# A transformer block whose first phase begins seven heads on half of the hidden dimension, with the shift joined later as a bias

## The chip, the cores and the metric

The kernel runs on one core of a Trainium2 chip. The metric is the device time of one execution in microseconds (us), lower is better. Every run of this document counts as fast by the rule that sorts slow executions out (no run was over 1.5% above the fastest of its kernel), so all comparisons are between fast runs. The differences here are a few tenths of a per cent, so the runs come in rounds of five, beside nine runs of the kernel before on the same chip.

Engines in the profile are PE (TensorE, matmuls), PEld (its weight loads), DVE (VectorE), ACT (ScalarE), POOL (GpSimd) and SP (which issues the loads here).

## The reference

One block of a transformer with modulation, in bf16: S = 2048 rows, D = 1024, 32 query heads on 4 key/value heads of 128, the last 512 keys only, and a gated FFN of 3584.

```python
mod = (silu(c) @ w_mod).reshape(1, 6, 1, -1)
sa, ca, ga, sb, cb, gb = ...                     # six vectors of D
h = layernorm(x) * (1 + ca) + sa                 # scale 1 + ca, shift sa
x = x + ga * (attention(h @ wq, k[-512:], v[-512:]) @ wo)
h = layernorm(x) * (1 + cb) + sb
x = x + gb * ((silu(h @ w_gate) * (h @ w_up)) @ w_down)
```

## The kernel before

The rows go in four chunks of 512. For each chunk and head there is a unit of three parts on PE: q (8 matmuls of 128x512), the scores S (4 of the same size, with the exponential on ACT), and the output O (16 of 130 columns, on the unit before). The steady unit takes 3.5 us, without a gap on PE. The change touches only what comes ahead of the first units: loading x, the scale (`ca1` = 1 + ca) and shift (`sa`), the first layernorm, and the q of the first heads.

```python
for tt in range(QT): load_x(tt)                  # 4 tiles of x, 256 KB each
for half in range(DH):                           # halves of D
    load_wm(1, half)                             # w_mod of the scale, 1 MB
    load_wm(0, half)                             # w_mod of the shift, 1 MB
    load_wq(0, 0, (half,))                       # Wq of heads 0-3, half of D, 1 KB rows
# ... K, V, then load_wq(0, 1): heads 4-7
warm(16)                                         # matmuls on constants, to raise the clock
# ... SiLU of c, on ACT and DVE

def mod_cols(vec, half, dst, add_one):           # 512 values of one vector
    ps = mm("mod_ps", (P, 4))
    for i in range(4):
        for dt in range(DT):                     # 32 matmuls with ONE moving column
            nc.tensor.matmul(ps[:, i:i + 1], lhsT=wm[:, dt, i * P:(i + 1) * P],
                             rhs=siluc[:, dt:dt + 1], start=(dt == 0), stop=(dt == DT - 1))
    # ... to dst on DVE

LEAD = 3
for t in range(QT):
    ln_stats(t); n = ln_norm(t, t % 2 == 0)      # statistics on DVE, norm on ACT or DVE
    # 8 transposes of n into PSUM (h0_ps)
    warm(2)
for half in range(DH):
    mod_cols(1, half, ca1, True)
    mod_cols(0, half, sa, False)
    for dt in range(4 * half, 4 * half + 4):     # h = n * ca1 + sa, out of PSUM
        ln_affine(("h1", 0), dt, h0_ps[half][:, dt % 4, :], ca1, sa, dt % 2 == 0)
    # this half's 4 of the 8 q matmuls, for LEAD heads
# ...
for k in range(NU + 1):                          # units
    # loads of Wq are issued 8 heads ahead
    emit_s(k); emit_q(k + LEAD); run_tasks(k); emit_o(k - 1)
```

No program order is forced on the engines in this phase, apart from the warm-up matmuls; a scheduler places the instructions. In the trace of before, the warm-up matmuls up to 5.7 us are 0.427 us apart from start to start, and those after it 0.216: that is the rise of the clock.

Of the kernel before, what the change touches and what calls it, by code (L numbers as in the profile page):

```python
# [8 lines left out]
ACT = mybir.ActivationFunctionType  # L9
# [579 lines left out]
def fast_path(ctx, tc, flag, A_x, A_k_cache, A_v_cache, A_wq, A_wo, B_x, B_w_gate, B_w_up,  # L589
# [41 lines left out]
    hpool = ctx.enter_context(tc.tile_pool(name="hT", bufs=4))  # L631
    pa_ = ctx.enter_context(tc.tile_pool(name="blkA", bufs=8))
    pb_ = ctx.enter_context(tc.tile_pool(name="blkB", bufs=7))
    pc_ = ctx.enter_context(tc.tile_pool(name="blkC", bufs=12))
    wk = ctx.enter_context(tc.tile_pool(name="work", bufs=2))
    sm = ctx.enter_context(tc.tile_pool(name="small", bufs=4))
    psp = ctx.enter_context(tc.tile_pool(name="psum", bufs=4, space=bass.MemoryType.PSUM))
# [28 lines left out]
    def load(out, in_):  # L666
        with nc.allow_non_contiguous_dma(reason="weight slice"):
            fetch(out=out, in_=in_)

    nc.scalar.preload_act_table_set("natural_log_exp_and_others")  # L670


# [16 lines left out]
    def load_wq(cc, hg, parts=(0, 1)):  # L689
        for i in parts:  # L690
            t = blkB("wq", [P, 4, 512])
            load(t, wq_v[:, 4 * i:4 * i + 4, hg * 512:(hg + 1) * 512])
            wq_tiles[(cc, hg, i)] = t

    for tt in range(QT):
        load_x(tt)
    for half in range(DH):
        load_wm(1, half)
        load_wm(0, half)
        load_wq(0, 0, (half,))  # L700
    kT = blkB("kT", [P, Hkv, W])
    for kv in range(Hkv):
        pin(nc.sync.dma_start_transpose(  # L703
# [2 lines left out]
    v_sb = const.tile([P, Hkv, WT, Dh + 32], BF16, name="v_sb")  # L706
    for kv in range(Hkv):
        load(v_sb[:, kv, :, 0:Dh], v_v[:, kv])
    nc.gpsimd.memset(v_sb[:, :, :, Dh:VN], 1.0)
    load_wq(0, 1)  # L710


    ident = const.tile([P, P], BF16, name="ident")
    make_identity(nc, ident)
    ones_bf = const.tile([P, P], BF16, name="ones_bf")
    nc.vector.memset(ones_bf, 1.0)
    eps_t = const.tile([P, 1], FP32, name="eps_t")
    nc.vector.memset(eps_t, eps)

    warm_w = const.tile([P, 512], BF16, name="warm_w")  # L720
    nc.gpsimd.memset(warm_w, 0.5)
    warm_ps = mm("warm_ps")

    def warm(n):
        for _ in range(n):
            tc.keep_in_program_order(
                nc.tensor.matmul(warm_ps, lhsT=ones_bf, rhs=warm_w, start=True, stop=True))

    warm(16)
    modT = const.tile([P, 4, DT], FP32, name="modT")  # L730
    sa, ca1, sb, cb1 = (modT[:, i, :] for i in range(4))
    ga_bc = const.tile([P, D], FP32, name="ga_bc")
    gb_bc = const.tile([P, D], FP32, name="gb_bc")


    ec = wk.tile([DT, P], FP32, name="ec", tag="f32", bufs=2)
    nc.scalar.activation(out=ec, in_=c_r, func=ACT.Exp, scale=-1.0)
    nc.vector.tensor_scalar(out=ec, in0=ec, scalar1=1.0, scalar2=None, op0=ALU.add)
    rc = wk.tile([DT, P], FP32, name="rc", tag="f32", bufs=2)
    nc.vector.reciprocal(out=rc, in_=ec)  # L740
    sil_r = const.tile([DT, P], BF16, name="sil_r")
    nc.vector.tensor_tensor(out=sil_r, in0=c_r, in1=rc, op=ALU.mult)
    sil_ps = mm("sil_ps", (P, DT), BF16)
    nc.tensor.transpose(sil_ps, sil_r, ident[0:DT, 0:DT])
    siluc = const.tile([P, DT], BF16, name="siluc")
    nc.vector.tensor_copy(out=siluc, in_=sil_ps)

    def mod_cols(vec, half, dst, add_one):
        wm = wm_tiles.pop((vec, half))
        ps = mm("mod_ps", (P, 4))  # L750
        for i in range(4):
            for dt in range(DT):
                nc.tensor.matmul(ps[:, i:i + 1], lhsT=wm[:, dt, i * P:(i + 1) * P],
                                 rhs=siluc[:, dt:dt + 1], start=(dt == 0), stop=(dt == DT - 1))
        nc.vector.tensor_scalar(out=dst[:, 4 * half:4 * half + 4], in0=ps,  # L755
                                scalar1=1.0 if add_one else 0.0, scalar2=None, op0=ALU.add)






# [144 lines left out]
            at(k + 11 + dt, ln_mod, key, dt, sc, sh)  # L907


    LEAD = 3  # L910
    qT = {}

    def put_q(g, q_ps):
        t = wk.tile([P, TCW], BF16, name="qT", tag="row", bufs=5)
        nc.vector.tensor_copy(out=t, in_=q_ps)  # L915
        qT[g] = t



    new_hT(("h1", 0))  # L920
    h0_ps = [big("h0_ps", (P, 4, TCW), BF16) for _ in range(2)]
    for t in range(QT):
        ln_stats(t)
        n = ln_norm(t, t % 2 == 0)
        for dt in range(DT):
            nc.tensor.transpose(h0_ps[dt // 4][:, dt % 4, t * P:(t + 1) * P],
                                n[:, dt * P:(dt + 1) * P], ident)
        warm(2)
    q0_ps = []
    for half in range(DH):  # L930
        mod_cols(1, half, ca1, True)
        mod_cols(0, half, sa, False)
        for dt in range(4 * half, 4 * half + 4):
            ln_affine(("h1", 0), dt, h0_ps[half][:, dt % 4, :], ca1, sa, dt % 2 == 0)
        if half == 0:
            q0_ps = [mm("q_ps") for _ in range(LEAD)]
        for n in range(4 * LEAD):
            dt, g = (4 * half + n // LEAD, n % LEAD) if half == 0 else (4 + n % 4, n // 4)
            nc.tensor.matmul(q0_ps[g],
                             lhsT=wq_tiles[(0, 0, dt // 4)][:, dt % 4, g * P:(g + 1) * P],  # L940
                             rhs=hT[("h1", 0)][:, dt, :], start=(dt == 0), stop=(dt == DT - 1))
    for g in range(LEAD):
        put_q(g, q0_ps[g])

    k_ld = []
    NSQ = 2 * 2 * (H // 4)
# [24 lines left out]
                                               accum_out=kk[:, i:i + 1]))  # L971

    def bound_mod():
        nc.vector.tensor_reduce(out=gd[:, 1:2], in_=kk, axis=AX.X, op=ALU.max)
        c2 = sm.tile([P, DT], FP32, name="c2", tag="c2", bufs=2)
        nc.vector.tensor_tensor(out=c2, in0=ca1, in1=ca1, op=ALU.mult)
        nc.vector.tensor_reduce(out=gd[:, 2:3], in_=c2, axis=AX.X, op=ALU.max)
        s2 = sm.tile([P, DT], FP32, name="s2", tag="c2", bufs=2)
        nc.vector.tensor_tensor(out=s2, in0=sa, in1=sa, op=ALU.mult)
        nc.vector.tensor_reduce(out=gd[:, 3:4], in_=s2, axis=AX.X, op=ALU.add)  # L980

    def bound_final():
        nc.vector.tensor_reduce(out=gd[:, 0:1], in_=sq, axis=AX.X, op=ALU.add)
# [30 lines left out]
    def emit_q(g):  # L1014
        cc, h = divmod(g, H)
        q_ps = mm("q_ps")
        for dt in range(DT):
            nc.tensor.matmul(q_ps,  # L1018
                             lhsT=wq_tiles[(cc, h // 4, dt // 4)][:, dt % 4,
                                                                 (h % 4) * P:(h % 4 + 1) * P],  # L1020
                             rhs=hT[("h1", cc)][:, dt, :], start=(dt == 0), stop=(dt == DT - 1))
        put_q(g, q_ps)

# [114 lines left out]
    for g in range(3, NU, 4):  # L1138
        at(g + 3, xpose_o, g // H, (g % H) // 4)
    for cc in range(1, NTC):  # L1140
        plan_ln((cc - 1) * H + (10 if cc == 1 else 2), ("h1", cc), ca1, sa)
    for cc in range(NTC):
        for q in range(NQ):
            s0 = cc * H + q * HQ + HQ + 5
# [25 lines left out]
    def emit_gu(cc, f):  # L1170
        fg, fi = divmod(f, 4)
        if fi == 0:
            guT[(cc, fg)] = blkA("guT", [P, 4, TCW])
        ps = big("gu_ps")
        for n, nm in enumerate(("wg", "wu")):
            for dt in range(DT):
                nc.tensor.matmul(ps[:, n, :],  # L1177
                                 lhsT=gu_w[(cc, fg, nm, dt // 4)][:, dt % 4, fi * P:(fi + 1) * P],
                                 rhs=hT[("h2", cc)][:, dt, :], start=(dt == 0),
                                 stop=(dt == DT - 1))  # L1180
        g = wk.tile([P, TCW], BF16, name="sg", tag="row", bufs=5)
        nc.scalar.activation(out=g, in_=ps[:, 0, :], func=ACT.Silu)  # L1182
        nc.vector.tensor_tensor(out=guT[(cc, fg)][:, fi, :], in0=ps[:, 1, :], in1=g, op=ALU.mult)  # L1183

# [5 lines left out]
    def emit_down(cc, dh, t, widths=(512,)):  # L1190
        row = (cc * QT + t) * P
        c0 = 0
        for w in widths:
            dsl = slice(dh * 512 + c0, dh * 512 + c0 + w)
            d_ps = mm("d_ps", (P, w))
            for f in range(FT):
                nc.tensor.matmul(d_ps, lhsT=guT[(cc, f // 4)][:, f % 4, t * P:(t + 1) * P],  # L1197
                                 rhs=wd_tiles[(cc, dh, f // 4)][:, f % 4, c0:c0 + w],
                                 start=(f == 0), stop=(f == FT - 1))
            r = wk.tile([P, w], FP32, name="f32", tag="f32", bufs=2)  # L1200
            nc.vector.tensor_tensor(out=r, in0=d_ps, in1=gb_bc[:, dsl], op=ALU.mult)  # L1201
            o = wk.tile([P, w], BF16, name="o_sb", tag="row", bufs=5)
            nc.vector.tensor_tensor(out=o, in0=r, in1=xt[cc * QT + t][:, dsl], op=ALU.add)
            nc.scalar.dma_start(out=out2d[row:row + P, dsl], in_=o)
            c0 += w
# [4 lines left out]

    stage["steps"] = True
    for k in range(NU + 1):
        if k % 4 >= 2 and 4 * (k // 4) + 8 < NU:
            g = 4 * (k // 4) + 8
            load_wq(g // H, (g % H) // 4, (k % 4 - 2,))
        if k < NU:
            emit_s(k)
        if k + LEAD < NU:
            emit_q(k + LEAD)
        if k == NU - 4:  # L1220
            load_gu(0, 0)
        run_tasks(k)
        if k >= 1:
            emit_o(k - 1)
# [63 lines left out]
```

## Time and profile before

| | before |
|---|---|
| median of the runs (first 3; all 6) | 1277.75; 1277.67 us |
| PE busy | 1255.9 of 1275.6 us |
| first q matmul starts | 15.74 us |
| end of the first head's O | 31.3 us |

First the page of the kernel before: PE's busy time, and the shares of the chain that ended last.

```profile
span 1275.6 us, 17906 instructions
...
PE 1255.9 (98%) x7396; PEld 640.6 (50%) x7537; DVE 606.9 (48%) x1325; ACT 333.7 (26%) x433; POOL 1.3 (0%) x10
...
## 4 chain that ended last, share of the span: by engine, by line
PE 96%; SPq 2%; issue 1%; DVE 1%; DMA 0%
```

PE bounds the kernel, and 2% of the chain lies on SP's queue, which issues the loads: early on, PE waited for weights. Where, the timeline of PE shows (start, length, line and operation, how many; in brackets the idle time before and what ended it).

```profile
15.74 1.46 PE L939 MATMUL q_ps<-hT,wq 128*128 128x512 bf16 x6 [1.06 <-ACT hT L852]
...
19.84 0.95 PE L753 MATMUL mod_ps<-siluc,wm 128*128 128x1 bf16 x32 [0.55 <-DMA wm<-in_w_mod_dram]
21.05 1.02 PE L1018 MATMUL q_ps<-hT,wq 128*128 128x512 bf16 x3 [0.26 <-DVE modT L755]
...
28.52 1.04 PE L1018 MATMUL q_ps<-hT,wq 128*128 128x512 bf16 x4 [0.25 <-DMA wq<-in_A_wq_dram]
...
32.02 1.89 PE L1018 MATMUL q_ps<-hT,wq 128*128 128x512 bf16 x8
...
785.48 1.67 PE L1197 MATMUL d_ps<-wd,guT 128*128 128x512 bf16 x7
...
1267.80 1.45 PE L1197 MATMUL d_ps<-wd,guT 128*128 128x128 bf16 x23
```

How to read it: a line's length includes the end of its last matmul, which the next line already overlaps (the line at 32.02 us is 1.89 us long, and the next O starts after 1.73), so rates are read from start to start. Eight 128x512 matmuls from 32.02 to 33.75 us (the next O) take 1.73 us, 0.216 each. From 32.02 us on the kernel is in its steady unit. The needed work done by then is 40 q, 12 S and 16 O matmuls, 12.1 us at the steady rates. The other 19.9 us are what this document calls the lead-in: all time at the start in which PE did no q, S or O. The last two lines, from two short stretches of the timeline (a group is cut off where the stretch begins or ends), are the first matmul of the down projection, and the last group of all, which ends at 1269.25 us. Some records of matmuls are missing in this trace, so its counts fall a little short.

### The profile page before, as it was taken

How to read it: one execution, taken by the hardware profiler on the slowest of the kernel's cores; microseconds unless marked ns; L12 is line 12 of the kernel's file. 1: busy time of each engine (PE TensorE's matmuls, PEld its weight loads, DVE VectorE, ACT ScalarE, POOL GpSimd, SP SyncE). 2: the span in 40 equal slices, each digit the busy share in tenths (PEclk: the TensorE clock that was granted, in tenths of full speed). 3: DMA queues.
4: the chain of work that ended last, by engine and by line, in shares of the span. 5: the costliest groups of instructions: out<-in, count | busy, mean ns of one | idle time of the engine just before them, and what ended most of it. 6: DMA issues, size and time to landing. Idle time of an engine off the chain costs nothing.

```text
span 1275.6 us, 17906 instructions
## 1 busy us (share of the span) xinstructions
PE 1255.9 (98%) x7396; PEld 640.6 (50%) x7537; DVE 606.9 (48%) x1325; ACT 333.7 (26%) x433; POOL 1.3 (0%) x10
## 2 busy tenths in 40 slices
PE   8999999999999999999999999999999999999997
PEld 4555555555555555555554444444444444444444
DVE  4575578867587755576654632321222112221212
ACT  4543334343343433333341111011100111011100
POOL 0000000000000000000000000000000000000000
PEclk9999999999999999999999999999999999999999
DMA  9988556685646563546465367426632565425711
GB/s 276 220 219 212 144 137 182 165 192 148 176 125 168 137 183 107 152 112 145 126 196 147 133 226 199 145 95 211 218 129 81 175 216 189 139 91 182 246 35 35
DMA packets 307868, 204.46 MB, mean 160 GB/s; under 512 B 145601, under 2 KB 305345, under 8 KB 307778
## 3 DMA queue, kind: packets, MB, share of 16 engines
q1 hardware_dynamic: 302866, 199.03, 55.0%
q10 hardware_dynamic: 4912, 4.20, 1.0%
q8 instruction: 61, 1.00, 0.3%
q14 instruction: 29, 0.24, 0.1%
HBM read 165.94 MB, written 4.21 MB: 133 GB/s over the span
## 4 chain that ended last, share of the span: by engine, by line
PE 96%; SPq 2%; issue 1%; DVE 1%; DMA 0%
PE gu_ps L1177 30%; PE a_ps L1095 17%; PE q_ps L1018 17%; PE d_ps L1197 15%; PE o_ps L1063 9%; PE s_ps L1031 8%; SPq L664 1%; SPq L703 1%; DMA wq<-in_A_wq_dram 0%; DVE junk L954 0%; DVE qT L915 0%; DVE junk L786 0%; DVE acc L1103 0%; DVE oq L1050 0%; DVE f L1201 0%
## 5 line engine op out<-in xcount | busy, mean ns | idle before, releaser
L1033 ACT ACTIVATE pT<-s_ps 128x1024 bf16<-128x1024 f32 x256 | 248.9, 1020 | 356.6 <-PE s_ps L1031 228.9
L1095 PE MATMUL a_ps<-wo,oT 128*128 128x512 bf16 x987 | 239.9, 379 | 2.0
L1018 PE MATMUL q_ps<-hT,wq 128*128 128x512 bf16 x999 | 236.7, 379 | 0.6 <-DVE modT L755 0.3
L1183 DVE TENSOR_TENSOR guT<-gu_ps,sg 128x512 bf16<-128x512 f32 x112 | 77.4, 691 | 286.4 <-ACT sg L1182 286.4
L1177 PE MATMUL gu_ps<-hT,wg 128*128 128x512 bf16 x875 | 209.7, 379 | 1.1
L1182 ACT ACTIVATE sg<-gu_ps 128x512 bf16<-128x512 f32 x112 | 66.9, 597 | 488.7 <-PE gu_ps L1177 483.0
L1197 PE MATMUL d_ps<-wd,guT 128*128 128x512 bf16 (+2 forms) x934 | 193.2, 366 | 0.9
L915 DVE CAST qT<-q_ps 128x512 bf16<-128x512 f32 x128 | 88.2, 690 | 158.5 <-PE q_ps L1018 157.7
L1177 PE MATMUL gu_ps<-hT,wu 128*128 128x512 bf16 x659 | 162.0, 379 | 0.7
L1095 PEld LDWEIGHTS <-oT 128*128 128x128 bf16 x1024 | 100.1, 98 | 120.6
L1018 PEld LDWEIGHTS <-wq 128*128 128x128 bf16 x1000 | 97.7, 98 | 118.2 <-DMA wq<-in_A_wq_dram 0.7
L1197 PEld LDWEIGHTS <-guT 128*128 128x128 bf16 x952 | 90.9, 98 | 103.0
L1063 PEld LDWEIGHTS <-pT 128*128 128x128 bf16 x2048 | 126.8, 98 | 31.0 <-issue 0.4
L1177 PEld LDWEIGHTS <-wg 128*128 128x128 bf16 x896 | 87.7, 98 | 105.5
L1063 PE MATMUL o_ps<-v_sb,pT 128*128 128x130 bf16 x2048 | 137.3, 220 | 0.1
L1031 PE MATMUL s_ps<-qT,kT 128*128 128x512 bf16 x467 | 129.3, 379 | 3.0 <-ACT pT L1033 0.6
L1177 PEld LDWEIGHTS <-wu 128*128 128x128 bf16 x672 | 65.7, 98 | 79.3
L1050 DVE TENSOR_TENSOR oq<-o_ps,rl 128x256 bf16<-128x256 f32 (+2 forms) x256 | 100.4, 419 | 3.8 <-issue 0.2
L1201 DVE TENSOR_TENSOR f<-d_ps,gb_bc 128x512 f32<-128x512 f32 (+2 forms) x34 | 22.4, 660 | 142.3 <-PE d_ps L1197 142.3
L1031 PEld LDWEIGHTS <-kT 128*128 128x128 bf16 x512 | 44.9, 98 | 31.5 <-issue 1.3
L1103 DVE TENSOR_TENSOR acc<-a_ps,acc 128x512 f32<-128x512 f32 x64 | 44.0, 688 | 34.3 <-PE a_ps L1095 34.3
L1177 PE MATMUL gu_ps<-hT,v_sb 128*128 128x512 bf16 x220 | 56.9, 379 | 0.2
(76 smaller groups left out, 400.2 us busy)
## 6 DMA issues: line engine op xcount, KB each, us to landing
wq<-in_A_wq_dram SPq DMA_DIRECT2D x64, 512.0 KB
wo<-in_A_wo_dram SPq DMA_DIRECT2D x64, 512.0 KB
wg<-in_B_w_gate_dram SPq DMA_DIRECT2D x56, 512.0 KB
wd<-in_B_w_down_dram SPq DMA_DIRECT2D x56, 512.0 KB
wu<-in_B_w_up_dram SPq DMA_DIRECT2D x42, 512.0 KB
v_sb<-in_B_w_up_dram SPq DMA_DIRECT2D x14, 512.0 KB
x<-in_A_x_dram SPq DMA_DIRECT2D x16, 256.0 KB
wm<-in_w_mod_dram SPq DMA_DIRECT2D x4, 1024.0 KB
```

The lines of the kernel that those rows point to most:

```text
L915: nc.vector.tensor_copy(out=t, in_=q_ps)
L1018: nc.tensor.matmul(q_ps, lhsT=wq_tiles[(cc, h // 4, dt // 4)][:, dt % 4, (h % 4) * P:(h % 4 + 1) * P], rhs=hT[("h1", cc)][:, dt, :], start ...
L1031: nc.tensor.matmul(s_ps[:, i, :], lhsT=kT[:, kv, j * P:(j + 1) * P], rhs=qT[g], start=True, stop=True)
L1033: nc.scalar.activation(out=p[:, 2 * jj:2 * jj + 2, :], in_=s_ps, func=ACT.Exp, scale=scale)
L1050: nc.vector.tensor_tensor(out=dst, in0=ps[:, s0:s0 + cnt, 0:Dh], in1=sc, op=ALU.mult)
L1063: nc.tensor.matmul(o_slot["ps"][:, s_, :], lhsT=pT[g][:, j, t * P:(t + 1) * P], rhs=v_sb[:, kv, j, 0:VN], start=(j == 0), stop=(j == WT - 1))
L1095: nc.tensor.matmul(a_ps, lhsT=oT[(cc, 2 * q + i)][:, hh % 4, t * P:(t + 1) * P], rhs=wo_tiles[(cc, q, dh, i)][:, hh % 4, :], start=(hh == ...
L1103: nc.vector.tensor_tensor(out=acc[(cc, t)][:, dsl], in0=a_ps, in1=acc[(cc, t)][:, dsl], op=ALU.add)
L1177: nc.tensor.matmul(ps[:, n, :], lhsT=gu_w[(cc, fg, nm, dt // 4)][:, dt % 4, fi * P:(fi + 1) * P], rhs=hT[("h2", cc)][:, dt, :], start=(dt ...
L1182: nc.scalar.activation(out=g, in_=ps[:, 0, :], func=ACT.Silu)
L1183: nc.vector.tensor_tensor(out=guT[(cc, fg)][:, fi, :], in0=ps[:, 1, :], in1=g, op=ALU.mult)
L1197: nc.tensor.matmul(d_ps, lhsT=guT[(cc, f // 4)][:, f % 4, t * P:(t + 1) * P], rhs=wd_tiles[(cc, dh, f // 4)][:, f % 4, c0:c0 + w], start=( ...
```

## The change

The intent is to give PE q matmuls earlier, and none to wait for. The shift is needed only as a vector added to q: (n·ca1 + sa)·Wq = (n·ca1)·Wq + sa·Wq. So h without its shift (`hs`) is multiplied first, for seven heads, the first half of D before the second; the shift's part is one bias per head, made by matmuls with one moving column. Wq of eight heads is then loaded before the shift's w_mod, in rows of 2 KB. Layernorm is spread differently, there are fewer warm-up matmuls, and the order of the first phase is fixed on every engine. A few small moves are left out of the diff below: among them, the next chunk's layernorm is planned five units earlier and the first load of the FFN's weights one unit earlier.

```diff
     for half in range(DH):
         load_wm(1, half)
-        load_wm(0, half)
-        load_wq(0, 0, (half,))
+        load_wq8(2 * half)                      # [P, 2, 8 heads]: 0.5 MB, 2 KB rows
+        load_wq8(2 * half + 1)
+    load_wm(0, 0)
+    load_wm(0, 1)
 ... K, V
-    load_wq(0, 1)
+    load_wq(0, 2)
-    warm(16)
+    warm(6)
 ... SiLU by ACT alone (Exp, Ln, Exp), siluc copied by ACT
+    warm(4)
-    LEAD = 3
+    LEAD = H0                                   # 7; row buffers 5 -> 9, blkC pool 12 -> 11
+    stats_0(0)                                  # DVE
+    act_sum(3)                                  # statistics of tile 3 on ACT, in two passes
+    stats_0(1)
+    xpose_0(0, ln_norm(0)); warm(4)             # all norms on DVE
+    act_squares(3); stats_0(2); rstd_0(3, 1.0 / D)
+    xpose_0(1, ln_norm(1)); warm(4)
+    n2 = ln_norm(2); n3 = ln_norm(3)
+    mod_cols(1, 0, ca1, True, (0,)); xpose_0(2, n2); xpose_0(3, n3)
+    mod_cols(1, 0, ca1, True, (1, 2, 3))
 ... hs = h0_ps * ca1, no shift: D tile 0 by ACT out of PSUM, the others copied
 ... out of PSUM by DVE in pairs and then scaled
+    def shift_cols(half):                       # bias of 7 heads, 28 one-column matmuls
+        for g in range(H0):
+            for i in range(4):
+                nc.tensor.matmul(ps[:, g:g + 1], lhsT=w0(g, 4 * half + i),
+                                 rhs=sa_bf[:, dt:dt + 1], start=(i == 0), stop=(i == 3))
 ... 7 heads x 4 D tiles of the first half; mod_cols(1, 1) within
+    for g in range(4): q0(g, range(4, DT))      # second half of D
+    sa_cols(0)                                  # 32 one-column matmuls: shift, first half
+    q0(4, range(4, DT))
+    shift_cols(0)                               # 28
+    sa_cols(1)                                  # 32
+    q0(5, range(4, DT))
+    shift_cols(1)                               # 28
+    q0(6, range(4, DT))
+    for g in range(4): put_q(g, q0_ps[g], bias_q[:, g:g + 1], g % 2 == 1)
 ... shift added to h in place, for the heads after the seventh
+    chain(first)                                # fixed order on each engine
 ... loads of Wq are issued 12 heads ahead instead of 8
```

## The prediction

> **What bounds the kernel now.** TensorE: the page shows PE busy 1255.9 of 1275.6 us, and the chain that ended last is 96% PE. In the PE timeline eight 128x512 matmuls take 1.73 us, 0.216 each[...]. Time is won only where PE does no needed matmul; for this change, in the first phase.
>
> **Its cost now.** The PE timeline reaches the steady unit of 3.5 us (S 0.86, q 1.73, O 0.91) at 32.0 us. Needed work done by then: 40 q, 12 score and 16 output matmuls = 8.6 + 2.6 + 0.9 = 12.1 us. The other 19.9 us are lead-in: warm-up matmuls, 128 modulation columns (32 in 0.94 us), transposes, idle time. The first q matmul starts at 15.7 us; PE waits around 20 us for w_mod and at 28.5 us for Wq by DMA.
>
> **What the change does.**
> - Loads: eight heads of Wq come before the shift's w_mod, so 7 MB instead of 6 stand ahead of K. At 386 GB/s (windows from 10 to 20 us), 2.7 us per MB, K, V and the next Wq land 2.7 us later, estimated 28 and 31 us. From wider rows I expect nothing: 1 KB rows already get 386 GB/s.
> - LN: one tile's statistics and the SiLU go to ACT, all norms to DVE (0.53 us against ACT's 1.24). I estimate the first q matmul at 12.3 us.
> - From there PE has 56 q matmuls (12.1 us), three modulation blocks (2.8) and 56 shift columns (new, 1.6 at 0.029 each). DVE copies h out of PSUM in two pieces of about 1.0 us, with 0.3 us scalings: about 1.3 us of PE waits between the first D tiles.
> - Seven heads are done at an estimated 30.3 us; eight bias evictions (0.69 us on DVE, about 0.6 on ACT) and four in-place affines delay the first scores and head 7 by 0.3 to 1 us. Lead-in becomes about 18.3 us.
>
> Nearly all of this is on PE's critical path. Afterwards the matmuls are the same; a lead of 7 heads changes only what runs early. One block fewer in the wo/wd pool should cost nothing: loads are issued about four units ahead.
>
> **Prediction:** 1275.7 us, 8 in 10 between 1273.2 and 1278.2. Faster by over 2%: 0.01; within 2%: 0.97; slower by over 2%: 0.02.
>
> **What would show the steps right or wrong.** First q matmul at 11.5 to 13 us; PE gaps of 0.5 to 0.8 us before the second and third D tile, then nearly none until 30 us; no wait for w_mod or Wq over 0.5 us; 1 to 3 us less lead-in than 19.9; from then on an unchanged offset between the traces to the end.
>
> **What would make it wrong.** (1) Fewer warm-up matmuls with gaps: PE may stay at the slow clock longer. Warm-up matmuls take 631 ns instead of 379 until about 5.6 us now[...]. Slow until 10 us or later would cost 1 to 3 us. (2) Fixed order per engine: one late wait (x's fourth tile on ACT, siluc) holds everything behind it. (3) K, V or heads 8 to 11 of Wq landing after 31 us: up to 2 us. (4) The longer lead and the smaller pool may delay the load queue and stall PE in the first chunk: 1 to 3 us.

The lead-in comes to about 18.3 us, 1.6 less than before's 19.9. Some of the terms are estimates: 1.0 us for a copy of h out of PSUM (in before's trace DVE takes 0.54 us for half as much), 0.3 for a scaling (0.54 us there for a norm of twice as much, out of SBUF), and 0.6 for an eviction on ACT (0.597 us there for another tile of 128x512). In the trace of after they took 0.69, 0.35 and about 0.68 us. The 386 GB/s are those of 10 to 15 us; the whole stretch from 10 to 20 us has 378.

## More of the kernel before

After the last matmul there is a tail, of additions and stores. In this view of stretches (busy time of each engine with instruction counts, mean granted clock, DMA share, GB/s), the line is that tail:

```profile
1269.25:1275.60 6.35, 0.00 (x0) 0.00 (x0) 0.58 (x2) 0.00 (x0) 0.00 (x0) 0.72 0.10 21
```

## The result, and the profile after

| | before | after |
|---|---|---|
| all runs | 1277.92, 1277.75, 1277.31, 1275.94, 1277.64, 1277.70 | 1273.63, 1277.58, 1274.38, 1278.22, 1276.21, 1274.32 |
| median | 1277.67 us | 1275.3 us |
| ratio of fast runs | | 0.9987 (95%: 0.9973 to 1.0002) |
| PE busy of span | 1255.9 of 1275.6 | 1262.7 of 1271.9 |

Ratios are the mean time of one kernel's fast runs over that of the other's of the same rounds, so not quite the ratio of the medians. The result is 2.4 us less by the medians.

The page of the kernel after; SP's queue is gone from the shares of the chain.

```profile
span 1271.9 us, 18166 instructions
...
PE 1262.7 (99%) x7587; PEld 641.2 (50%) x7587; DVE 609.0 (48%) x1335; ACT 334.9 (26%) x439; POOL 1.3 (0%) x10
...
PE 98%; DVE 1%; DMA 0%; issue 0%; ACT 0%; ACTq 0%
```

The timeline of PE of the kernel after:

```profile
11.89 0.81 PE L1013 MATMUL q_ps<-hs,wq 128*128 128x512 bf16 x3
13.16 0.81 PE L1013 MATMUL q_ps<-hs,wq 128*128 128x512 bf16 x3 [0.47 <-DVE hs L993]
14.15 3.18 PE L1013 MATMUL q_ps<-hs,wq 128*128 128x512 bf16 x14 [0.18 <-DVE hs L993]
17.17 0.94 PE L773 MATMUL mod_ps<-siluc,wm 128*128 128x1 bf16 x32
17.97 5.34 PE L1013 MATMUL q_ps<-hs,wq 128*128 128x512 bf16 x24
23.15 0.94 PE L773 MATMUL mod_ps<-siluc,wm 128*128 128x1 bf16 x32
23.95 1.02 PE L1013 MATMUL q_ps<-hs,wq 128*128 128x512 bf16 x4
24.81 0.84 PE L1024 MATMUL sh_ps<-sa_bf,wq 128*128 128x1 bf16 x28
25.91 0.94 PE L773 MATMUL mod_ps<-siluc,wm 128*128 128x1 bf16 x32 [0.26 <-DVE bias_q L1027]
...
35.48 1.03 PE L1153 MATMUL s_ps<-qT,kT 128*128 128x512 bf16 x4
...
782.90 2.32 PE L1319 MATMUL d_ps<-wd,guT 128*128 128x512 bf16 x10
...
1265.83 0.83 PE L1319 MATMUL d_ps<-wd,guT 128*128 128x128 bf16 x12
```

The steady state begins at 35.48 us here, with 72 q, 8 S and 16 O matmuls done, 18.2 us of work. The lead-in is 35.5 − 18.2 = 17.3 us, 2.6 less than before. No wait for w_mod or Wq is left. The terms of the 17.3 are: first q at 11.89; three blocks of 32 modulation columns, 0.80 each from start to start; two of 28 shift columns, 0.70 each, and the 0.26 us wait; 0.62 + 0.34 us lost from start to start between the first D tiles; about 0.25 before the first scores. They add up to 17.2. A one-column matmul takes 25 ns from start to start (32 in 0.80 us).

The offset is rigid. The down projection's first matmul is at 785.48 and 782.90 us, 2.58 apart; the last matmul ends at 1269.25 and 1266.67, again 2.58. The 1230 us between have neither added nor lost anything. The two spans, however, differ by 3.7 us. The remaining 1.1 is the tail: this stretch of the kernel after is 1.1 us shorter than that shown of before.

```profile
1266.67:1271.90 5.23, 0.00 (x0) 0.00 (x0) 0.58 (x2) 0.00 (x0) 0.00 (x0) 1.00 0.11 25
```

All the later traces, of both kernels and of all experiments, have tails of 5.1 to 5.4 us; only the first trace of before has 6.35, where the last store's issue took 1.35 us instead of 0.34. The 1.1 us belong to that execution and not to the change.

One thing did not fit: the runs after spread over 4.6 us, from 1273.63 to 1278.22, where the prediction had expected one time. The run's mean granted clock goes with it: 1.000, 0.999 and 1.000 in the three fastest, 0.998 in the one at 1276.21, and 0.996 in the two slowest. The experiments turned to that.

### The profile page after: what moved, and what is told of

Read it like the earlier page. It is cut to its first block, busy times and chain, and to the rows that moved or that the text cites. A ratio compares the mean times of both kernels' runs of the same rounds, so it can differ in the third digit from the quotient of the medians.

```text
span 1271.9 us, 18166 instructions
## 1 busy us (share of the span) xinstructions
PE 1262.7 (99%) x7587; PEld 641.2 (50%) x7587; DVE 609.0 (48%) x1335; ACT 334.9 (26%) x439; POOL 1.3 (0%) x10
## 4 chain that ended last, share of the span: by engine, by line
PE 98%; DVE 1%; DMA 0%; issue 0%; ACT 0%; ACTq 0%
PE gu_ps L1299 30%; PE a_ps L1217 17%; PE q_ps L1142 16%; PE d_ps L1319 15%; PE o_ps L1185 9%; PE s_ps L1153 9%; PE q_ps L1013 1%; DVE st L833 0%; DVE junk L1076 0%; PE mod_ps L773 0%; DMA x<-in_A_x_dram 0%; PE h_ps L948 0%; DVE qT L934 0%; DVE hT L873 0%; DVE junk L804 0%
## 5 line engine op out<-in xcount | busy, mean ns | idle before, releaser
L1142 PE MATMUL q_ps<-hT,wq 128*128 128x512 bf16 x968 | 229.2, 379 | 0.0
L934 DVE CAST qT<-q_ps 128x512 bf16<-128x512 f32 x121 | 83.6, 691 | 147.9 <-PE q_ps L1142 147.6
L1142 PEld LDWEIGHTS <-wq 128*128 128x128 bf16 x968 | 94.7, 98 | 114.1
L1153 PE MATMUL s_ps<-qT,kT 128*128 128x512 bf16 x512 | 131.9, 379 | 0.1
```

Source lines behind the costliest of these rows:

```text
L934: nc.vector.tensor_copy(out=t, in_=q_ps)
L1142: nc.tensor.matmul(q_ps, lhsT=w, rhs=hT[("h1", cc)][:, dt, :], start=(dt == 0), stop=(dt == DT - 1))
L1153: nc.tensor.matmul(s_ps[:, i, :], lhsT=kT[:, kv, j * P:(j + 1) * P], rhs=qT[g], start=True, stop=True)
```

## The experiments

The expectations name the theories that stood against each other at the time. In short, one (A; its description in r1's record is cut, as no trace showed it) was that the gaps between warm-up matmuls and transposes before 12 us let PE's clock drop in some runs. When that fell, a second (A2) took its place: the stretch from 23 to 29 us, where most of PE's instructions are one-column matmuls, lets it drop. The rivals were the arrival of the loads, the shares of layernorm, and the wider rows as the source of the gain or the spread.

To tell how busy a stretch is, I worked out a "streamed share", an estimate, from the starts and widths of the matmuls in each trace: columns streamed, at 0.213 us for 512 (half of the 0.427 us from start to start that the warm-up matmuls take in before and after until the clock rises, at 5.72 and 5.59 us; at full clock the traces have 0.216), as a share of a window. A one-column matmul adds next to nothing to it, though the profile counts it as busy. The windows are those of the trace's own clock records, whose changes lie 3.413 us or a multiple of it apart: 3.41 us in r2 (29.77 to 33.18 us), and 1266.345 us, 371 times as much, from the rise at 5.59 us in after to the next change. The traces of before and of r5 to r11 lack up to 2% of the matmul records (r6 has 7447, after 7587). Where the order of the matmuls shows that one is missing in a window, it is put back, and the text says so.

### r1_after_again: the same kernel, five runs on another chip

No edit.

> The changed kernel, unaltered. Its six first runs spread over 1273.6 to 1278.2 us, while five of the six of before lie within 1277.3 to 1277.9, and the two slow runs of the changed kernel show a mean granted clock of 0.996 against 1.000. Theory A [...]: the spread comes back, time falls as the mean clock rises, and a trace of a slow run shows 512-column matmuls of about 630 ns somewhere before 30 us. Theory B (noise of the chip, not of this kernel): the runs of before in this call spread as widely.

Measured: 1274.48, 1274.44, 1275.35, 1274.52, 1275.23; median 1274.52 against 1276.48 of before; ratio 0.9985 (0.9972 to 0.9999). The spread did not come back. In its trace the first q matmul starts at 12.77 us, 0.88 later than in the first one, because the last tile of x landed 0.88 later (7.12 against 6.24 us) and the scale's w_mod 0.83 later (10.26 against 9.43); the last matmul ends 0.87 later too. So the loads' arrival, which varies between executions, passes one to one into the time. That accounts for 0.9 us of spread and not for 4.6.

### r2_dense_warm: more warm-up matmuls where PE idled early

```diff
-    warm(4)                    # after siluc
+    warm(7)
...
     xpose_0(0, ln_norm(0))
-    warm(4)
+    warm(6)
```

> The changed kernel with five more warm-up matmuls in gaps where TensorE only waits (7 instead of 4 after the SiLU transpose, 6 instead of 4 after the first tile's transposes). They should delay nothing: first q matmul at 11.9 us as in the changed kernel. Theory A: no slow runs, all near 1273.6 to 1274.4 and clock 0.999 to 1.000. Theory B: the same spread as the changed kernel.

Measured: 1277.30, 1274.60, 1276.33, 1274.38, 1275.40; median 1275.4, ratio 0.9988 (0.9974 to 1.0001). The first q matmul came at 13.08 us and not at the expected 11.9, because the last tile of x landed at 7.44 us against 6.24 in after. The profiled run was the slowest, and it caught the drop. By stretch, PE is shown busy for 3.15 of 3.41 us (86 matmuls) in the first line, and at half clock in the second, with 10 matmuls in place of 16:

```profile
26.36:29.77 3.41, 3.15 (x86) 2.49 (x83) 1.15 (x6) 0.00 (x0) 0.00 (x0) 1.00 0.85 184
29.77:33.18 3.41, 3.41 (x10) 1.19 (x9) 3.38 (x9) 1.34 (x2) 0.00 (x0) 0.50 0.83 287
```

The timeline of PE shows what was in the first of them:

```profile
27.10 0.94 PE L773 MATMUL mod_ps<-siluc,wm 128*128 128x1 bf16 x32 [0.26 <-DVE bias_q L1027]
27.90 1.02 PE L1013 MATMUL q_ps<-hs,wq 128*128 128x512 bf16 x4
28.76 0.84 PE L1024 MATMUL sh_ps<-sa_bf,wq 128*128 128x1 bf16 x28
29.47 1.60 PE L1013 MATMUL q_ps<-hs,wq 128*128 128x512 bf16 x4
```

Between 26.36 and 29.77 us PE streams four 512-column matmuls and the equal of one and a half more: a share of 35%. The longest idle time is 0.26 us. Then the clock is halved for exactly one window. The early gaps were filled and the drop came all the same, 17 us later: theory A falls, A2 is formed. In the first trace of after the same stretch fell differently into the windows (40% in the one from 22.66 us) and kept its clock; the least favourable window, starting at 23.19 us, would have had 26%. The windows do not follow the kernel's start (one begins at 22.66 us in after, 22.94 in r2, 23.07 in r4, 24.28 in r12), so of their possible starts 1.45 of 3.41 us would give under 35%, the share at which r2 dropped: an estimate of 43% of the runs, if every such window drops. Five runs of r1 without a drop have then a chance of 6% (one of the five, with a mean clock of 0.998, may have had one). Over the 11 runs of the unaltered kernel (6 and 5), two have a mean clock of 0.996, which is more half clock (0.4% lost of 1276 us is about 10 us at half clock) than the idle tail of 5.1 to 6.35 us can hold; 0.998 can be one window or a longer tail.

### r3_stats_on_dve: tile 3's statistics back on DVE

```diff
-    act_sum(3)
...
-    act_squares(3)
-    rstd_0(3, 1.0 / D)
     xpose_0(1, ln_norm(1))
+    stats_0(3)
```

> Undoes the split of the layer norm: the fourth tile's statistics are taken by DVE again, after the second tile's norm. If the layer norm chain is critical and the rest of the first phase is bound by TensorE, the first q matmul moves from 11.9 to about 12.6 us and the last matmul by the same 0.6 to 0.7 us. If instead arrivals by DMA bound the phase later on, the later start is absorbed and the end does not move.

Measured: 1275.59, 1274.83, 1274.53, 1277.28, 1275.31; median 1275.31, ratio 0.9990 (0.9976 to 1.0004). The first q matmul starts at 13.13 us, 1.24 later than in after, and the end of the first O is 1.24 later: what comes in front of the first q passes one to one. In this trace PE's clock rose only at 10.39 us, against 5.59 in after, so that four warm-up matmuls took twice the time (1.71 us from start to start of the lines, against 0.86 at full clock), and w_mod came late as well (10.87). In r6 and r10, which leave the statistics on ACT, the clock rose as late (10.65 and 10.31) and the first q matmul came at 13.13 and 13.04 us. So the late clock is enough for the 1.24 us, and no cost of this edit can be seen; the expected 0.6 to 0.7 us was not shown.

### r4_five_heads: five heads instead of seven

```diff
-    H0 = 7
+    H0 = 5
...
-    q0(5, range(4, DT))
     shift_cols(1)
-    q0(6, range(4, DT))
```

> Five heads begun ahead instead of seven. Theory 1 (TensorE bounds the phase, the number of heads matters little): 16 fewer shift columns save 0.5 us, less work to hide the bias behind costs about as much, so the last matmul moves by less than 0.7 us. Theory 2 (seven heads are needed to cover the arrival of w_mod, K, V and Wq): a wait of 1 us or more on DMA appears before 32 us and the kernel is 1 to 3 us slower.

Measured: 1278.12, 1277.36, 1276.86, 1278.24, 1276.12; median 1277.36, ratio 1.0003 (0.9989 to 1.0017). The gain is gone, but for neither theory's reason as it was put: there is no long wait for a load. With the two heads' matmuls gone, the one-column blocks stand closer together; the window from 23.07 to 26.49 us streams 30%, and the clock is half for two windows, to 33.31 us. In the timeline of PE eight q matmuls take 3.37 us to the next start, 0.42 each:

```profile
26.79 0.69 PE L1024 MATMUL sh_ps<-sa_bf,wq 128*128 128x1 bf16 x20 [0.46 <-DVE sa_bf L1033]
27.34 3.57 PE L1140 MATMUL q_ps<-hT,wq 128*128 128x512 bf16 x8
30.71 1.06 PE L1151 MATMUL s_ps<-qT,kT 128*128 128x512 bf16 x2
```

So in this trace the number of heads matters also as filling between the one-column matmuls. Why the clock stayed low for a second window, in which PE streamed 77% at half clock, is not shown.

### r5_interleaved and r6_clumped: the same matmuls, in another order

These two tell A2 from its rivals directly. The 35% of A2 is an estimate from three windows: those of r2 (35% streamed) and r4 (30%), each followed by half clock, and that of after (40%), which was not. The work is the same, only the order of the one-column and the 512-column matmuls differs. r5 puts a 512-column matmul after every 8 to 28 columns; r6 puts the four blocks of columns one after another.

```diff
-    sa_cols(0)                          # r5
-    q0(4, range(4, DT))
-    shift_cols(0)
-    sa_cols(1)
-    q0(5, range(4, DT))
-    shift_cols(1)
+    sa_cols_mixed(0, 8)                 # a q0 matmul of head 3 after every 8 columns
+    q0(4, range(4, DT))
+    shift_cols_mixed(0, 14)             # heads 5 and 6 after every 14, 16, 28
+    sa_cols_mixed(1, 16)
+    shift_cols_mixed(1, 28)
```

```diff
-    sa_cols(0)                          # r6
     q0(4, range(4, DT))
+    q0(5, range(4, DT))
+    sa_cols(0)
     shift_cols(0)
     sa_cols(1)
-    q0(5, range(4, DT))
     shift_cols(1)
```

> The changed kernel with the same matmuls in another order after 22 us: the one-column matmuls (shift's modulation and shift columns) alternate with the 512-column ones of heads 3 to 6, so that no stretch of 3.4 us is mostly one-column work. Theory A2, from the traces so far: TensorE's clock halves at the end of a 3.41 us window when it streamed less than about 35% of that window; the window's phase differs from run to run; in the changed kernel starts over 1.45 us of 3.41 give such a window (its worst streams 26%), so some 4 runs in 10 lose 1.7 or 3.4 us. Then here all five runs keep the clock (0.999 to 1.000) and lie within 1 us of each other, at the fast end of the changed kernel on this chip. Theory B (the drop has another cause, or is random): slow runs as often as before.

> The opposite: all one-column matmuls of the shift stand together, about 3.8 us with hardly any 512-column matmul. Theory A2: nearly every run has a window under 35%, so at least four of five lose 1.7 or 3.4 us beside about 0.5 us of new waits: 1276 to 1279 us, clock under 0.999 in the trace and a half-clock stretch after 27 us. Theory B: no more slow runs than the changed kernel, about 0.5 us slower.

Measured, r5: 1274.57, 1275.39, 1273.83, 1274.89, 1274.85; median 1274.85 against 1277.26 of before, ratio 0.9984 (0.9970 to 0.9998). Its mean clock is 0.999 or 1.000 in all five runs, as expected; they span 1.56 us, though, where 1 us had been expected. r6: 1278.29, 1278.14, 1279.13, 1277.83, 1277.73; median 1278.14, ratio 1.0011 (0.9997 to 1.0025), with a clock of 0.996 to 0.998 in all five. The order alone is worth 3.3 us by the medians, and the ranges do not touch. In r6 the timeline of PE has

```profile
26.12 0.94 PE L773 MATMUL mod_ps<-siluc,wm 128*128 128x1 bf16 x32
27.52 0.85 PE L1024 MATMUL sh_ps<-sa_bf,wq 128*128 128x1 bf16 x28 [0.46 <-DVE sa_bf L1033]
28.63 0.94 PE L773 MATMUL mod_ps<-siluc,wm 128*128 128x1 bf16 x32 [0.26 <-DVE bias_q L1027]
30.03 0.85 PE L1024 MATMUL sh_ps<-sa_bf,wq 128*128 128x1 bf16 x28 [0.46 <-DVE sa_bf L1033]
```

and, by stretch, two windows:

```profile
27.70:31.10 3.40, 2.60 (x88) 2.36 (x87) 1.63 (x7) 0.00 (x0) 0.00 (x0) 1.00 0.95 265
31.10:34.50 3.40, 3.40 (x9) 1.21 (x8) 3.37 (x9) 1.35 (x2) 0.00 (x0) 0.50 0.29 98
```

PE is "busy" for 2.60 of 3.40 us in the first, and streams 11% of it. (The records alone give 6%: the first of head 6's four matmuls, after the 28 columns that end at 30.73 us, is missing and put back here.) The second runs at half clock, which costs half of it, 1.7 us. The clumping also brings two more waits of 0.46 us for the shift's small copies, because nothing is left to do meanwhile. In the two profiled executions the last matmuls end 3.9 us apart: 1.7 by the clock, 0.9 by those waits, 0.7 by a later first q (13.13 against 12.43 us), and 0.6 by a later wait in the FFN. The later first q is another thing: in this execution the clock rose at 10.65 us instead of 5.59 as in after, though x and w_mod arrived alike (6.26 and 9.42 against 6.24 and 9.43 us), and the first q came 1.24 later than after's. That is the first danger which the prediction named, and it is real, but r3, r8 and r10 show it too, and nothing in the start of r6 was edited. A2 stands.

### r7_before_fast_ln and r11_before_fast_ln2: the other half alone

Is the faster layernorm the gain? Here the kernel before gets after's layernorm, SiLU and fixed order, with its own loads, q and shift. r11 is r7 with fewer warm-ups.

```diff
+    def chain(start): ...               # both, on the kernel before
-    for t in range(QT):
-        ln_stats(t)
-        n = ln_norm(t, t % 2 == 0)
+    stats_0(0); act_sum(3); stats_0(1); xpose_0(0, ln_norm(0)); warm(2)
+    act_squares(3); stats_0(2); rstd_0(3, 1.0 / D); xpose_0(1, ln_norm(1)); warm(2)
+    n2 = ln_norm(2); n3 = ln_norm(3); xpose_0(2, n2); xpose_0(3, n3)
-    warm(16)                            # r11 only
+    warm(6)
...
+    warm(4)                             # r11 only, after siluc
```

> The kernel before with one part of the change: SiLU and the fourth tile's statistics on ACT, all norms on DVE, fixed order; loads, three heads ahead and the shift in h as before. Theory 1 (the start of before is held by arrivals: w_mod's third and fourth blocks at 16 and 20 us, Wq of heads 4 to 7 at 28.5): the transposes finish 2 us earlier, but O of the first head and the end move by less than 0.5 us. Theory 2 (the layer norm was the bottleneck): 1.5 to 2 us faster than before.

> Repeats the fast layer norm in the kernel before, with 6 + 4 warm-up matmuls as in the changed kernel instead of 16, because the 16 held back the SiLU transpose until 7.5 us, and with it, by the fixed order on ACT, every rstd. Theory 1 (arrivals hold the start of before): transposes end near 11 us instead of 13.1 to 13.5, first q matmul between 13.5 and 14.5, but the end is no earlier than in before by more than 0.5 us (1276 or more). Theory 2 (the layer norm was the bottleneck): 1.5 us or more faster than before. A half-clock stretch is likely (64 one-column matmuls in a row) and would add to the time.

Measured, r7: 1278.38 to 1278.77, median 1278.55, ratio 1.0014 (1.0001 to 1.0028). It failed as a test. The copy of siluc stands on ACT ahead of the layernorm's square roots, and the SiLU's transpose waited behind 16 warm-up matmuls:

```profile
7.47 0.17 PE L755 MATMUL sil_ps<-ident,sil_r 8*128 8x8 bf16 x1
8.92 0.62 PE L935 MATMUL h_ps<-ident,xn 128*128 128x128 bf16 x8 [1.27 <-DVE xn L845]
```

The first of these lines is at 4.28 us in after. The kernel fixes ACT's order, so the square roots, and with them the norms on DVE, stood behind that copy: the first transposes of layernorm started at 8.92 us, after a wait of 1.27 us for DVE's norm, against 6.91 us in after. The transposes ended at 13.07 us and nothing was gained. Two half-clock windows came on top (the trace's mean clock is 0.997, and single q matmuls stand 0.43 us apart from 23.67 to 26.23 us).

r11 mends that: 1276.73, 1277.17, 1277.66, 1279.26, 1277.50; median 1277.5, ratio 1.0009 (0.9996 to 1.0023). The timeline of PE of r11:

```profile
14.20 1.86 PE L985 MATMUL q_ps<-hT,wq 128*128 128x512 bf16 x4 [1.06 <-ACT hT L864]
...
19.79 0.95 PE L765 MATMUL mod_ps<-siluc,wm 128*128 128x1 bf16 x32 [0.42 <-DVE c L1023]
```

The first q is 1.5 us earlier than in before, but the shift's second w_mod still lands at 19.7 us, and the block that needs it starts at 19.79 against 19.84. The layernorm alone only makes PE wait there, with a lower streamed share: windows at 13% and 26%, each followed by a window at half clock. A faster start is worth nothing until the loads that come next are out of the way. The joint effect of both can't be split more finely from these runs, because the clock windows lie on top of them.

### r8_shift_loads_early: only the order of the loads undone

```diff
         load_wm(1, half)
+        load_wm(0, half)
         load_wq8(2 * half)
         load_wq8(2 * half + 1)
-    load_wm(0, 0)
...
-    load_wm(0, 1)
```

> The changed kernel with the shift's two w_mod blocks loaded where before had them, ahead of Wq of the same half. Theory 1 (the order of loads is what lets the earlier start and the fill work): Wq's first pieces land at about 14 instead of 11.1 us and its last at about 23 instead of 17.9, so the first q matmul moves to about 14 us and a further wait appears before the second half of D: 2 to 4 us slower than the changed kernel in runs of the same clock. Theory 2 (all 7 MB must arrive before the scores anyway): within 0.7 us.

Measured: 1281.39, 1281.72, 1281.14, 1282.05, 1280.08; median 1281.39, ratio 1.0035 (1.0021 to 1.0049). Its timeline of PE:

```profile
14.44 4.58 PE L1012 MATMUL q_ps<-hs,wq 128*128 128x512 bf16 x19 [1.51 <-DMA wq<-in_A_wq_dram]
...
23.54 0.76 PE L1012 MATMUL q_ps<-hs,wq 128*128 128x512 bf16 x2 [2.00 <-DMA wq<-in_A_wq_dram]
24.92 4.33 PE L1012 MATMUL q_ps<-hs,wq 128*128 128x512 bf16 x14 [0.62 <-DMA wq<-in_A_wq_dram]
```

These waits add up to 4.1 us, and two half-clock windows (from 23.85 and 34.09 us) come with them. This is the largest single effect: the order of the loads is what keeps PE fed while seven heads' weights arrive.

### r10_1kb_rows: narrower rows

```diff
-        load(t, wq_v[:, 2 * i:2 * i + 2, 0:8 * P])
+        for j in range(2):
+            load(t[:, :, 512 * j:512 * j + 512], wq_v[:, 2 * i:2 * i + 2, 512 * j:512 * j + 512])
```

> The changed kernel with each 0.5 MB load of Wq's first eight heads split in two loads with 1 KB rows, in the same place. Theory 1 (bandwidth does not depend on 1 or 2 KB rows here): the last Wq piece lands within 0.5 us of 17.3 to 18 us, time as the changed kernel at the same clock. Theory 2 (2 KB rows matter): Wq, and with it the first half of D, lands 1 to 2 us later.

Measured: 1275.44, 1274.92, 1276.43, 1277.37, 1275.03; median 1275.44, ratio 0.9994 (0.9980 to 1.0007). PE waits nowhere for the first eight heads' weights; its only wait for Wq is the 0.2 us before 33.93 us, for heads 8 to 11. The width of the rows makes no clear difference here.

### r9_best: what the runs point to

An even interleaving, the second D tile scaled by ACT out of PSUM, and DVE's copies in another order so that they do not stand in front of the tiles PE waits for.

```diff
+    for dt in range(2):                 # ACT scales D tiles 0 and 1 from PSUM
+        nc.scalar.activation(out=hs[0][:, dt, :], in_=h0_ps[0][:, dt, :], ...)
-    nc.vector.tensor_copy(out=h10[:, 0:2, :], in_=h0_ps[0][:, 0:2, :])
-    h_scale(1)
     nc.vector.tensor_copy(out=h10[:, 2:4, :], in_=h0_ps[0][:, 2:4, :])
     h_scale(2); h_scale(3)
+    nc.vector.tensor_copy(out=h10[:, 0:2, :], in_=h0_ps[0][:, 0:2, :])
... act_sum(3) after stats_0(1); q0 matmuls after every 8, 14, 8 and 28 columns
```

> The interleaved kernel with three more changes of order: the one-column matmuls alternate with 512-column ones more evenly (no window of 3.41 us under 40%); ACT takes the fourth tile's sum after the second tile's rstd, so a late arrival of that tile holds up less; ACT makes h's first two D tiles straight from PSUM while DVE copies the next two, so the two waits of 0.47 and 0.18 us (0.6 and 0.3 with the pipeline) before D tiles 1 and 2 shrink to one of about 0.4. If the accounts from the traces are right: first q matmul near 12 us, O of the first head 0.5 to 1 us earlier than in the interleaved kernel for the same arrival of x, no half-clock stretch, five runs within 1273.0 to 1274.6. If not (the waits only move to w_mod's last block, which lands at 24.6 to 25.3 us): same as the interleaved kernel, 1274.8.

Measured: 1274.12, 1275.07, 1274.90, 1274.14, 1274.16; median 1274.16 against 1277.11, ratio 0.9983 (0.9969 to 0.9997). Its five runs lie within 1 us and its trace has no half clock before the tail; the least favourable window of the whole first phase would stream 37%. The timeline of PE has the two waits between D tiles at

```profile
13.23 0.81 PE L1013 MATMUL q_ps<-hs,wq 128*128 128x512 bf16 x2 [0.19 <-ACT hs L997]
14.34 3.18 PE L1013 MATMUL q_ps<-hs,wq 128*128 128x512 bf16 x14 [0.30 <-DVE hs L993]
```

against 0.47 and 0.18 in after. That is little; its best run (1274.12) is no better than the best of after (1273.63). Two runs lie above the expected 1273.0 to 1274.6, and against r5 (ratio 0.9984) no gain can be told. What it should gain over after is the lack of slow runs; five runs can't show that by themselves, since the five of r1, of the unaltered kernel, lie within 1 us too.

### r12_before_again: does the kernel before drop too?

No edit; five runs of the kernel before.

> The kernel before, unaltered, for a second trace of it. Its times over four chips fall in two groups, 1275.7 to 1276.5 and 1276.9 to 1277.9. In the first trace (1277.4 us) the stretch from the end of the last matmul to the end of the span is 6.35 us, in all eleven other traces 5.15 to 5.4. Theory 1: the groups are this tail; a trace of the lower group shows a tail near 5.2 us and the last matmul still near 1269.3 us, so the true gain of the change at full clock is the 2.6 us by which its last matmul ends earlier. Theory 2: the groups are a half-clock window in the first phase, of which the first trace shows none; then a trace of the upper group shows one, and a trace of the lower group would have its last matmul clearly before 1269 us.

Measured: 1277.50, 1276.50, 1277.99, 1276.20, 1276.04; median 1276.5, ratio to the other nine runs of itself 1.0002. The profiled run, one of the upper group, caught a drop, in the wait for the shift's w_mod. The first line is the timeline of PE, the two after it are stretches:

```profile
21.31 1.86 PE L1018 MATMUL q_ps<-hT,wq 128*128 128x512 bf16 x4 [0.25 <-DVE modT L755]
```

```profile
17.46:20.87 3.41, 2.59 (x66) 1.94 (x64) 0.67 (x4) 0.00 (x0) 0.00 (x0) 1.00 1.42 250
20.87:24.28 3.41, 3.16 (x16) 1.14 (x13) 1.57 (x5) 1.56 (x2) 0.00 (x0) 0.50 0.99 200
```

The window before streams 28%. The last matmul ends at 1270.49 us, 1.24 later than in the first trace of before; the other part of the 1.7 us is taken up by the wait for Wq that came at 28.5 us there. So the two groups of times that before has (about 1275.5 to 1276.6, and 1276.9 to 1278.0) have at least two causes: this drop, and the longer tail of the first trace, which had no drop.

## Why the prediction was right

**The bound and the place of the gain: right.** PE's chain grew from 96% to 98%; all of the gain in the pair of traces is in the first 36 us, and the offset between them stays at 2.58 us from there to the last matmul.

**The start: right.** The first q matmul came at 11.89 us where 12.3 was predicted, but that trace is of the fastest of the six runs. In the eight other traces with the changed kernel's order of loads it was 12.2 to 13.1, when x or w_mod came later or the clock rose later.

**The loads: right.** No wait for w_mod or Wq is left in after. K's pieces land at 25.8 to 27.3 us, V's by 30.4 and the next Wq at 31.9 and 33.3, where 28 and 31 were estimated; PE waited for none of them. r8 shows the other side: with the shift's w_mod first, 4.1 us of waits.

**Seven heads, the columns and the waits: right in kind, most a little too large.** Modulation 2.4 us (predicted 2.8), shift columns 1.4 (1.6), with a wait of 0.26 beside them that was not foreseen, waits between D tiles 0.96 from start to start (1.3), delay of the scores about 0.25 (0.3 to 1). The columns were mis-sized because I divided a line's length, with its drain, by its count: 0.94 / 32 = 0.029, where start to start gives 0.025. The lead-in was 17.3 us and not 18.3, which alone would have put the time 1 us lower, near the 1273.6 to 1274.4 of the three fastest runs. This too is the fastest run's: in the trace of r1 all is 0.88 us later, which makes the lead-in 18.2.

**What brought the median back up was not foreseen at its place.** The prediction feared a late rise of the clock through fewer warm-ups. That happens (r6: 1.24 us), in four of the ten traces whose kernel begins with 6 + 4 warm-up matmuls and in none of the other four, which begin with 13 or 16; that is too few to call the warm-ups the shown cause. The mean granted clock does not tell of it (r3 and r10 have 1.000). The larger loss is a drop of the clock in the stretch of one-column matmuls, to which the change adds 56 and which it puts close to the 64 of the shift: r6 against r5 shows that it is their order, and r2 that it is not the early gaps. Each window at half clock costs 1.7 us (half of 3.41). The two slowest runs after, with a clock of 0.996, would lie at about 1274.2 and 1274.8 with two windows (3.4 us) taken off: an estimate from the clock, as these runs have no trace. That the median of 1275.3 fell so close to the predicted 1275.7 is therefore partly luck: terms that were estimated too large hid a loss that was not foreseen at its place. Which of the two losses by the clock is the more frequent is not known: of the five traces with after's order of columns (after, r1, r2, r3, r10) two have the late rise and one the drop.

**The tail.** Of the 3.7 us between the two profiled spans, 1.1 are the tail of one execution of before, and no gain. Whoever takes the difference of two profiled spans for the effect would have read 3.7.

**The rest.** Rows of 2 KB bring nothing that can be seen (r10), as predicted. No cost of the smaller pool or of the longer lead can be seen: the offset between the traces is 2.58 us at the first FFN matmul too (668.07 and 665.49 us), where all attention units are done. Five heads (r4) lose the gain, through the clock.

**Open.** The share of layernorm alone can't be told (r3, r7, r11 all had clock windows or late arrivals on top). Traces of r2, r3 and r6 lose another 0.5 to 1 us later, r2 and r6 with a single wait of 0.8 and 0.6 us in the FFN; I did not look into it. How often the unaltered kernel drops is known from few runs (two of eleven by their clock, perhaps four).

## What to carry to other kernels

When PE is 98% busy, count the time at the start in which it does no needed work: in the pair of traces here, what was taken off there (2.58 us) was kept to the end. Put the loads in the order in which PE can use them first, and move out of the front whatever can join later as a small bias. But a stretch of tiny matmuls was followed here by half clock, even where the profile showed PE busy (2.60 of 3.40 us in r6, with 11% streamed), so put large matmuls between them (in r5 the clock was then 0.999 or 1.000 in all five runs), and look at each run's granted clock, and at when it rose, before you explain a spread.

## What these traces measured of PE's clock

- Stretches at half clock before the tail lasted 3.41 us (r2, r6, r12) or 6.83 us (r4, from 26.49 to 33.31 us). They began after windows that streamed 11 to 36% of their time, with no idle gap over 0.5 us in r2 and r6 (the 11% is the stretch of r6). After windows at 40% and more at full clock it stayed there, and at 35 to 36% it went either way (kept in r3 and r10, lost in r2 and r8; for r10 one missing matmul, at 25.1 us, is put back, without which it would be 29%). The shares are estimates from matmul starts, on one core and with bf16. They show no exact limit, and not why the clock falls.
- The one-column matmuls took 25 ns each from start to start. The profile counts them as busy (PE 2.60 of 3.40 us in r6), while the streamed share was 11% and the next window ran at half clock.
- In four of fourteen traces the clock rose only at 10.2 to 10.7 us, though warm-up matmuls began at 1.6 us, with a gap of 0.5 to 0.9 us before the first transposes; in the others it rose at 4.2 to 7.3 us. Counted as above, but with 0.427 us for 512 columns at half clock, the earlier windows of those four streamed 53 to 72%, and the clock stayed low after them; after windows of 75% and more it rose, except after the one of 77% in r4.
